# Block loads behind weight loads, a weight sum and a unit's loads in other places, unit 0's bonus work in other levels

## The chip, the core and the metric

The kernel runs on one core of a Trainium2 chip. A core has five engines that work side by side, each through its own instructions in order: TensorE (PE, matrix products into PSUM), VectorE (DVE), ScalarE (ACT), GpSimd (POOL) and SyncE (SP), which here only issues DMAs. Semaphores tie them together. An instruction that waits holds up everything behind it on its engine, and a DMA that waits holds up SP's queue in the same way. The metric is the time of one execution on the device, in microseconds (us), as the median of several runs.

## What is computed

The reference is an RWKV6 attention block followed by a two-layer network with SiLU between the layers, cut here to its core:

```python
for t in range(S):                                   # B, H, S, D = 4, 8, 768, 48
    cur = einsum('bhd,bhe->bhde', u[None] * k[t], v[t])
    y[t] = einsum('bhd,bhde->bhe', r[t], state + cur)
    state = w[t][..., None] * state + einsum('bhd,bhe->bhde', k[t], v[t])
x = y as (3072 tokens, 384)
h = x @ w_in                                         # w_in: 384 x 2048
out = (h * sigmoid(h)) @ w_out                       # w_out: 2048 x 384
```

All data are float32. The recurrence over time is replaced by products inside chunks of 128 tokens, with a state that is carried from chunk to chunk.

## The kernel before

*Units.* The sequence has 6 chunks of 128 tokens, and each is done for two pairs of batches: 12 units, `i` = 0 to 11. The first two (`NTOK = 2`) are special: their inputs come in token by token and are turned on TensorE (`turn_in` L350, then copies L358 to L362), the others come in blocks (`load_blocks`, L106, four DMAs each, twelve calls for a unit) and are turned on VectorE (L338). Two units' inputs fit in `raw`, so the loads for unit `i + 2` go into the room that unit `i` has finished with.

*One unit.* In each of seven levels TensorE makes score products (`scores` or `burst`, L527), VectorE keeps those under a mask (`keep_masked`, L537; for three of them ScalarE copies instead, L556), VectorE multiplies the queries in place (`grow_queries`, L473, or `prepare`, L595), GpSimd the keys (`grow_keys`, L491) and the products of `w` (`product`, L386), and ScalarE moves the odd keys (L461). The queries of a level are overwritten only after the products of that level have read them, and the next level's products need the new ones. The diagonal is a bonus: sums of `r*k*u` (`bonus` L406 to L410, `bonus_sum` L415 and L419) are brought into place (`bonus_spread`: L436 on TensorE in the first two units, in the others by small DMAs into `diag`, L425, ScalarE copies L441 and L443 and a shuffle L444) and written into the scores by VectorE (`bonus_write`, L450, two instructions, `e` = 0 and 1). `reverse_v` reverses `v` of the second batch (L378 on TensorE and a copy L379, later a shuffle L381). Then `y` (L665), `turn_apart` (L628), `dense_x` or `move_x` (L703 with copies L705, or DMAs L715) and `update` (L679) end the unit. In unit 0 the sums of `bonus_spread` lie in `p_w`, a PSUM room that `tail_weight` (L203) uses as well.

*The network.* `up` (L756) makes a piece of the hidden layer from `xt` and `w_in_sb` into `p_h` (two rooms), ScalarE applies SiLU (L762) into `gt`. For the first unit `down` (L775) multiplies with `w_out` as it is. From the second unit on the product is done in seven quarter-size products (`quarter`, L819 and L828), which need sums of `gt` (`sums`, L801) and four sums of quarters of `w_out` (`weight_sums` 0 to 3, L793). `weight_sums(3)` overwrites a quarter of `w_out_sb` that quarter product 5 of unit 1 is the first to need.

*Weights.* Sixteen pieces are loaded (L178) into places that serve several of them, split in two parts on ScalarE (`head_weight` L195 and L197, `tail_weight` L203), joined on VectorE (`join_weight`, L214 and L215) and added on GpSimd (`add_weight`, L227). `join_weight(i)` also issues the load of the piece that takes the place over. Pieces 0 to 5 are loaded at the start, 6 to 11 are issued by the joins of 0 to 5.

*Order.* No scheduler decides: the order on every engine is the order in which the program calls its steps. `do(...)` calls a list of steps. For units 0 and 1 these lists are written by hand (L866 and after); from unit 3 on `mix(i)` returns fourteen groups of steps, and between groups come the steps of the network for the unit before (`ROOM` says how many after each group). `mix` also appends the block loads of unit `i + 2` and the values of unit `i + 1` to the groups from number 3 on, evenly. `beat(n)` issues `n` transposes whose result nobody reads.

Of the kernel before, what the change touches and what calls it, by code (L numbers as in the profile page):

```python
# [38 lines left out]
def kernel(  # L39
# [11 lines left out]
    nc = tc.nc  # L51
# [16 lines left out]
    NTOK = 2  # L68
# [650 lines left out]
    def both(fn, i, *args):  # L719
        return [(fn, i, b, *args) for b in range(NB)]  # L720

    def block_loads(i):
        return [(load_blocks, i, name, g) for name in "wkr" for g in range(4)]

    def mix(i):

        groups = [[*both(turn, i, "w"), (product, i, 0)],
                  [*both(turn, i, "k"), *both(turn, i, "r"), (odd_ones, i)], [(start_levels, i), (prepare_keys, i, 1)],
                  [(prepare, i, 1), *[(product, i, l) for l in range(1, NL)]],
                  [(burst, i, 1), (keep_level, i, 1)], [(keep_level, i, 2), (go_on, i, 2)],  # L730
                  [(prepare, i, 3), (reverse_v, i), (bonus, i, 0)],
                  [(burst, i, 3), (keep_level, i, 3), (bonus_sum, i, 0), (bonus, i, 1), (bonus, i, 2)],
                  [(keep_level, i, 4), (go_on, i, 4)],
                  [(prepare, i, 5), (bonus_sum, i, 1)] + ([(load_rk, i + 1)] if i + 1 < len(units) else []),
                  [(burst, i, 5), (keep_level, i, 5)], [(keep_level, i, 6), (go_on, i, 6), (bonus_spread, i), (bonus_write, i)],
                  both(turn_k, i), [*both(y_state, i), *both(y, i), *both(update, i), (move_x, i)]]

        loads = block_loads(i + NSLOT) if i + NSLOT < len(units) else []
        if i + 1 < len(units):
            loads.insert(len(loads) // 2, (load_values, i + 1))  # L740
        behind = groups[3:]
        for at, group in enumerate(behind):
            group += loads[at * len(loads) // len(behind):(at + 1) * len(loads) // len(behind)]
        return groups
# [89 lines left out]
    def ups(i):  # L834

        steps = [[(up, i, m)] for m in range(FC // 2)]
        for m in range(FH // 2 - 1):

            steps[FH // 2 + 1 + m].append((sums, i, m))
        steps[-1].append((sums, i, FH // 2 - 1))  # L840
        return steps

    def downs(i):
        return [[(quarter, i, x)] for x in range(7)]

    def do(*steps):
        for fn, *args in steps:
            fn(*args)
# [7 lines left out]
    def back(fn, i, *args):  # L856
# [7 lines left out]

    blocks = block_loads(2)
    others = {1: [(clear, 0), (beat, 6)], 2: [(turn, 1, 0, "r"), (head_weight, 0), (beat, 2)],  # L866
              3: [(turn, 1, 1, "r"), (head_weight, 1), (beat, 2)], 4: [(turn, 1, 1, "w"), (reverse_v, 0)],
              5: [(bonus_spread, 0), (bonus_write, 0), (turn, 1, 0, "w")], 6: [*both(turn_in, 1, "k"), *blocks[0:4], (tail_weight, 0)]}
    for l in range(1, NL):
        do((scores, 0, l), *[(grow_keys, 0, l + 1)] * (l + 1 < NL), *others[l])  # L870

    do((bonus, 1, 0), (bonus, 1, 1), (bonus, 1, 2), *both(y, 0), (turn_apart, 0), (join_weight, 0), (add_weight,),
       *blocks[4:8], (product, 1, 0), (tail_weight, 1), (turn, 1, 0, "k"), (join_weight, 1), (dense_x, 0, 0), (turn, 1, 1, "k"),
       (dense_x, 0, 1), (grow_queries, 1, 0), (odd_ones, 1), (tail_weight, 2), *both(turn_k, 0), (head_weight, 2),
       *blocks[8:12], (start_keys, 1, nc.gpsimd, True), (add_weight,), (up, 0, 0), (join_weight, 2),
       (start_keys, 1, nc.gpsimd, False), (add_weight,), (tail_weight, 3), (odd_keys, 1, 1), (head_weight, 3), (grow_keys, 1, 1),
       (scores, 1, 1, (join_weight, 3)), (add_weight,), (up, 0, 1), (tail_weight, 4), (grow_keys, 1, 2), (head_weight, 4),
       (up, 0, 2))


    others = {1: [], 2: [(bonus_sum, 1, 0), (bonus_sum, 1, 1), (load_rk, 2), *both(update, 0)],
              3: [(bonus_spread, 1), (reverse_v, 1), (clear, 1), (load_values, 2)]}

    def piece(i):
# [3 lines left out]
    for m in range(1, 4):  # L888
# [7 lines left out]
    blocks = block_loads(3)  # L896

    others = {0: [(up, 1, 1), (down, 0, 0, 0), *both(turn, 2, "k"), (product, 2, 0), (product, 2, 1)],
              1: [(up, 1, 2), *both(turn, 2, "r"), *[(product, 2, l) for l in range(2, NL)], *blocks[0:3]],
              2: [(down, 0, 0, 1), (odd_ones, 2), (start_keys, 2, nc.gpsimd, True), (grow_queries, 2, 0), *blocks[3:6]],  # L900
              3: [(up, 1, 3), (start_keys, 2, nc.gpsimd, False), (reverse_v, 2), *blocks[6:9]], 4: [(level, 2, 1), (up, 1, 4), *blocks[9:12]],
              5: [(down, 0, 0, 2), (up, 1, 5), (weight_sums, 0)]}
# [5 lines left out]
    blocks = block_loads(4)  # L908
# [10 lines left out]
    for i in range(3, len(units)):  # L919
        steps = downs(i - 2) + ups(i - 1)  # L920
        groups = mix(i)
        if i == NTOK + 1:

            groups[4].append((weight_sums, 3))
        for group, room in zip(groups, ROOM):
            do(*group)
            for step in steps[:room]:
                do(*step)
            steps = steps[room:]
# [32 lines left out]
```

## Time and profile before

| | |
|---|---|
| median of 11 runs | 649.8 us (649.3 to 651.99) |
| profiled execution | 649.36 us, of which the span from the first to the last instruction is 647.6 us |
| instructions | 12887 |
| granted TensorE clock | 1.00 of full speed |
| DMA | 49.21 MB, mean 76 GB/s |

The times in stages, in us (stretch; busy time of TensorE, VectorE, ScalarE, GpSimd):

| stretch | what runs | PE | DVE | ACT | POOL |
|---|---|---|---|---|---|
| 8 to 36 | unit 0 | 26.37 | 22.88 | 21.60 | 23.40 |
| 36 to 127 | units 1 and 2, weights, first of the network | 90.93 | 78.16 | 59.02 | 65.98 |
| 127 to 145 | start of unit 3 | 16.79 | 16.19 | 3.42 | 11.66 |
| 145 to 175 | rest of unit 3 | 29.63 | 16.04 | 7.64 | 9.47 |
| 175 to 647.6 | units 4 to 11 and the end | 469.39 | 294.85 | 107.94 | 166.35 |

A line of the timeline gives start, duration, engine, source line, operation, what is written and read, and in square brackets how long the engine stood idle before and what released it. A line of the waits gives engine, tile and line, the releaser, and the idle time in total, its number and the longest. An engine that is not the last to end may stand idle at no cost. Matmul ends are modelled, so that a matmul group's listed duration reaches a little into the next group.

### The profile page before, as it was taken

What the parts mean: (1) busy time and instruction counts of PE and PEld (TensorE: products, weight loads), DVE (VectorE), ACT (ScalarE), POOL (GpSimd) and SP (SyncE); (2) the same over time, 40 slices, a digit from 0 to 9 for tenths busy, and PEclk for the clock granted to TensorE, in tenths of its full rate; (3) what the DMA queues carried; (4) which work ended last, traced back from release to release, by engine and by line L of the source; (5) the groups of instructions that cost most, each with busy time, mean ns of one, the idle gap of its engine ahead of it and who ended that gap; (6) DMA issues with size and microseconds to landing.
All of it is one profiled execution on the core that took longest, in us unless ns stands there. A gap on an engine that the chain in (4) does not pass through costs nothing.

```text
span 647.6 us, 12887 instructions
## 1 busy us (share of the span) xinstructions
PE 639.4 (99%) x4878; PEld 578.5 (89%) x4878; DVE 433.4 (67%) x737; ACT 203.7 (31%) x408; POOL 282.4 (44%) x356
## 2 busy tenths in 40 slices
PE   8999999999999999999999999999999999999998
PEld 7888876889899899899899899899899989989997
DVE  7879789886487577586586686576576766751031
ACT  6797972212221321330321232231222222131120
POOL 6898388475055154244434426416416505510000
PEclk9999999999999999999999999999999999999999
DMA  9957954444534413514513513523431022000000
GB/s 228 276 94 180 271 126 51 88 78 69 97 53 77 85 36 64 98 30 66 95 29 66 99 26 58 100 33 51 85 62 38 26 50 50 26 3 25 25 0 25
DMA packets 201134, 49.21 MB, mean 76 GB/s; under 512 B 188912, under 2 KB 195952, under 8 KB 201072
## 3 DMA queue, kind: packets, MB, share of 16 engines
q1 hardware_dynamic: 199488, 47.79, 36.2%
q10 hardware_dynamic: 1584, 0.59, 0.4%
q8 instruction: 39, 0.64, 0.4%
q14 instruction: 23, 0.19, 0.1%
HBM read 39.52 MB, written 4.72 MB: 68 GB/s over the span
## 4 chain that ended last, share of the span: by engine, by line
PE 89%; DVE 4%; SPq 2%; POOL 2%; DMA 1%; issue 1%; ACT 1%; POOLq 0%; DVEq 0%; ACTq 0%
PE p_h L756 36%; PE p_o L819 31%; PE p_sc L527 6%; PE p_m L527 3%; PE p_m L775 3%; PE p_m L665 3%; PE p_m L652 3%; PE p_m L639 1%; SPq L106 1%; PE p_sc L679 1%; DMA raw<-in_r_dram 1%; POOL tk L491 1%; DVE score L537 1%; PE p_m L703 0%; DVE tr L473 0%
## 5 line engine op out<-in xcount | busy, mean ns | idle before, releaser
L756 PE MATMUL p_h<-xt,w_in_sb 128*128 128x256 f32 x1152 | 258.5, 382 | 1.1 <-POOL tk L507 0.7
L756 PEld LDWEIGHTS p_h<-xt,w_in_sb 128*128 128x128 f32 x1152 | 215.8, 190 | 33.1 <-POOL tk L507 0.9
L762 ACT ACTIVATE gt<-p_h 128x512 f32<-128x512 f32 x93 | 55.4, 596 | 223.6 <-PE p_h L756 223.5
L491 POOL TENSOR_TENSOR tk<-tk,tw 128x256 f32<-128x256 f32 x144 | 103.1, 739 | 21.3 <-ACT tk L461 15.2
L537 DVE COPY_PREDICATED score<-mask,p_sc 128x512 f32<-128x512 int8 x78 | 64.1, 884 | 60.5 <-PE p_sc L527 60.2
L819 PE MATMUL p_o<-w_out_sb,gt 128*128 128x192 f32 x528 | 90.5, 328 | 0.8 <-DVE w_out_sb L793 0.8
L819 PE MATMUL p_o<-own,temps 128*128 128x192 f32 x528 | 90.3, 328 | 0.4 <-DVE temps L828 0.4
L819 PEld LDWEIGHTS p_o<-w_out_sb,gt 128*128 128x128 f32 x528 | 85.8, 190 | 2.0 <-DVE w_out_sb L793 1.1
L819 PEld LDWEIGHTS p_o<-own,temps 128*128 128x128 f32 x528 | 85.8, 190 | 1.8 <-DVE temps L828 0.7
L684 POOL TENSOR_TENSOR state<-state,tw 128x512 f32<-128x512 f32 x16 | 19.3, 1225 | 119.1 <-PE p_m L652 119.1
L386 POOL TENSOR_TENSOR tw<-tw 128x256 f32<-128x256 f32 (+6 forms) x83 | 38.2, 460 | 56.6 <-DVE tw L338 52.7
L801 DVE TENSOR_TENSOR temps<-gt 128x256 f32<-128x256 f32 x88 | 44.3, 503 | 21.5 <-ACT gt L762 21.5
L461 ACT COPY tk<-tk 128x256 f32<-128x256 f32 x60 | 24.6, 411 | 81.0 <-PE p_sc L527 36.4
L527 PEld LDWEIGHTS p_sc<-tr,tk 48*128 48x128 f32 x640 | 39.2, 186 | 12.1 <-issue 9.1
L473 DVE TENSOR_TENSOR tr<-tr,tw 128x512 f32<-128x512 f32 x53 | 46.0, 869 | 3.3 <-POOL tk L491 1.0
L527 PE MATMUL p_sc<-tr,tk 48*128 48x128 f32 x640 | 47.1, 285 | 0.7 <-POOL tk L491 0.6
L408 POOL TENSOR_TENSOR ruk<-tokens_rk 128x768 f32<-128x768 f32 x10 | 18.6, 1858 | 66.7 <-DVE own_sums L415 66.7
L595 DVE TENSOR_TENSOR tr<-tr,tw 128x512 f32<-128x512 f32 x29 | 39.3, 1354 | 1.3
L537 DVE COPY_PREDICATED score<-mask,p_m 128x512 f32<-128x512 int8 x54 | 35.4, 704 | 0.0
L819 PE MATMUL p_o<-w_out_sb,temps 128*128 128x192 f32 x176 | 30.4, 326 | 0.0
L597 ACT COPY tr<-tr 128x512 f32<-128x512 f32 x29 | 18.4, 634 | 37.3 <-DVE tr L473 36.4
L507 POOL TENSOR_TENSOR tk<-tk,tw 128x128 f32<-128x128 f32 x44 | 29.2, 699 | 1.7 <-ACT tk L497 1.7
(144 smaller groups left out, 734.5 us busy)
## 6 DMA issues: line engine op xcount, KB each, us to landing
w_out_sb<-in_moe_w_in_dram SPq DMA_DIRECT2D x6, 768.0 KB, 6.7
tokens_rk<-in_r_dram SPq DMA_DIRECT2D x20, 192.0 KB, 3.4
tokens_rk<-in_k_dram SPq DMA_DIRECT2D x20, 192.0 KB, 3.9
w_out_sb<-in_moe_w_out_dram SPq DMA_DIRECT2D x4, 768.0 KB, 5.4
own<-in_moe_w_out_dram SPq DMA_DIRECT2D x4, 768.0 KB, 6.8
xt<-yt SPq DMA_DIRECT2D x60, 48.0 KB, 2.0
raw<-in_w_dram SPq DMA_DIRECT2D x80, 32.0 KB, 2.2
raw<-in_k_dram SPq DMA_DIRECT2D x80, 32.0 KB, 2.3
```

The lines of the kernel that those rows point to most:

```text
L386: engine.tensor_tensor(out=up, in0=t[:, :, 0::2], in1=t[:, :, 1::2], op=ALU.mult)
L461: nc.scalar.copy(out=keys(i, X[(l + 1) % 2] * L + c, [4 * c, blocks], [c, 2], [1, c]), in_=keys(i, NP * L + c, [4 * c, blocks], [NP * L + ...
L473: nc.vector.tensor_tensor(out=odd, in0=odd, in1=tw[i][l][:, :, 0::2][:, :, :, None].to_broadcast([128, Q, L >> (l + 1), c]), op=ALU.mult)
L491: nc.gpsimd.tensor_tensor(out=out, in0=have, in1=odd_products(i, l, b, *blocks), op=ALU.mult)
L507: engine.tensor_tensor(out=keys(i, X[1] * L + 3 * b, [4, n], [1, 1]) if own else have, in0=have, in1=odd_products(i, 0, b, [4, n], skip=2 ...
L527: nc.tensor.matmul(bass.AP(tensor=s_p.tensor, offset=s_p.offset, ap=[s_p.ap[0], [apart * L // 2, 2], [1, L // 2]]), lhsT=tk[i][rows, X[l % ...
L537: nc.vector.copy_predicated(out=dst, mask=masks[l][:, :, None].to_broadcast([128, NB, NP, ni, c]), data=sc[e].rearrange("p (b q) (i c) -> ...
L595: nc.vector.tensor_tensor(out=new[:, :, :, 1, :], in0=old[:, :, :, 1, :], in1=tw[i][l][:, :, 0::2][:, :, :, None].to_broadcast([128, Q, L ...
L756: nc.tensor.matmul(p_h[:, a, :], lhsT=w_in_sb[:, c, f * 128:(f + 1) * 128], rhs=xt[i][:, c, :], start=(c == 0), stop=(c == KC - 1))
L762: nc.scalar.activation(out=gt[i, m], in_=p_h, func=AF.Silu)
L801: nc.vector.tensor_tensor(out=out, in0=one, in1=two, op=op)
L819: nc.tensor.matmul(p, lhsT=left(f), rhs=right[:, f, :], start=(f == 0), stop=(f == FH - 1))
```

## The change

Five edits, all of them of places in the order:

1. In unit 0, `bonus_spread(0)` is called in level 3 instead of 5, in the place of a `beat` of two transposes, which goes. The two instructions of `bonus_write(0)` are called one in level 4 and one in level 5, where both were in level 5. `reverse_v(0)` goes from level 4 to level 5, ahead of the second of them.
2. The turns of unit 1: `turn(1, 0, "w")` goes from level 5 to level 6, `turn_in(1, 0, "k")` from level 6 to a place behind `y` of unit 0; the turn-outs of "k" change places, `s` = 1 now comes first.
3. The block loads of unit 2 for "k" and "r" are called later: "k" after the third join of weights, "r" after the piece in the next level. So weight loads 7 to 10 come ahead of them on SP's queue.
4. `mix(3)` puts the loads of unit 5 and the values of unit 4 behind the groups from 10 on, not from 3 on. `mix` of later units stays as it was.
5. `weight_sums(3)` is called second in group 4 of `mix(3)`, between `burst(3, 1)` and `keep_level(3, 1)`, and no longer last.

The number of DMAs and the work of VectorE, ScalarE and GpSimd stay the same. A blank line in `mix` moves the lines from there on by one.

```diff
@@ mix @@
             loads.insert(len(loads) // 2, (load_values, i + 1))
-        behind = groups[3:]
+
+        behind = groups[3 if i > NTOK + 1 else 10:]
         for at, group in enumerate(behind):
@@ unit 0, levels 1 to 6, and unit 1 @@
     others = {1: [(clear, 0), (beat, 6)], 2: [(turn, 1, 0, "r"), (head_weight, 0), (beat, 2)],
-              3: [(turn, 1, 1, "r"), (head_weight, 1), (beat, 2)], 4: [(turn, 1, 1, "w"), (reverse_v, 0)],
-              5: [(bonus_spread, 0), (bonus_write, 0), (turn, 1, 0, "w")], 6: [*both(turn_in, 1, "k"), *blocks[0:4], (tail_weight, 0)]}
+              3: [(turn, 1, 1, "r"), (bonus_spread, 0), (head_weight, 1)], 4: [(turn, 1, 1, "w"), (bonus_write, 0, [0])],
+              5: [(reverse_v, 0), (bonus_write, 0, [1])], 6: [(turn, 1, 0, "w"), (turn_in, 1, 1, "k"), *blocks[0:4], (tail_weight, 0)]}
...
-    do((bonus, 1, 0), (bonus, 1, 1), (bonus, 1, 2), *both(y, 0), (turn_apart, 0), (join_weight, 0), (add_weight,),
-       *blocks[4:8], (product, 1, 0), (tail_weight, 1), (turn, 1, 0, "k"), (join_weight, 1), (dense_x, 0, 0), (turn, 1, 1, "k"),
+    do((bonus, 1, 0), (bonus, 1, 1), (bonus, 1, 2), *both(y, 0), (turn_in, 1, 0, "k"), (turn_apart, 0), (join_weight, 0), (add_weight,),
+       (product, 1, 0), (tail_weight, 1), (turn, 1, 1, "k"), (join_weight, 1), (dense_x, 0, 0), (turn, 1, 0, "k"),
        (dense_x, 0, 1), (grow_queries, 1, 0), (odd_ones, 1), (tail_weight, 2), *both(turn_k, 0), (head_weight, 2),
-       *blocks[8:12], (start_keys, 1, nc.gpsimd, True), (add_weight,), (up, 0, 0), (join_weight, 2),
+       (start_keys, 1, nc.gpsimd, True), (add_weight,), (up, 0, 0), (join_weight, 2), *blocks[4:8],
...
-    others = {1: [], 2: [(bonus_sum, 1, 0), (bonus_sum, 1, 1), (load_rk, 2), *both(update, 0)],
+    others = {1: blocks[8:12], 2: [(bonus_sum, 1, 0), (bonus_sum, 1, 1), (load_rk, 2), *both(update, 0)],
@@ unit 3 @@
-            groups[4].append((weight_sums, 3))
+            groups[4].insert(1, (weight_sums, 3))
```

## The prediction

> **What bounds the kernel now.** I read the page's busy times, then TensorE's waits, then the timelines round each wait that the change touches.
>
> ```profile
> PE 639.4 (99%) x4878; PEld 578.5 (89%) x4878; DVE 433.4 (67%) x737; ACT 203.7 (31%) x408; POOL 282.4 (44%) x356
> ```
>
> TensorE is busy 639.4 of 647.6 us, so 8.2 us of idle time are all that reordering can win, apart from matmuls that are dropped. The waits of TensorE (total us, times, longest) name part of it:
>
> ```profile
> PE p_o L819 <- DVE w_out_sb L793: 0.8, 1, 0.8
> PE p_h L756 <- POOL tk L507: 0.7, 1, 0.7
> ...
> PE p_o L819 <- DVE temps L828: 0.4, 1, 0.4
> PE p_h L756 <- ACT gt L762: 0.4, 1, 0.4
> ```
>
> These four lie at 144.54, 36.05, 136.03 and 173.74 us. From 181 us to the end there are none, so the change is decided before that. The timeline of unit 0 (start us, us, engine):
>
> ```profile
> 20.51 0.44 PE L854 MATMUL p_m<-ident 128*128 128x128 f32 x2
> 20.88 1.16 PE L527 MATMUL p_sc<-tr,tk 48*128 48x128 f32 x16
> ...
> 22.75 1.33 DVE L537 COPY_PREDICATED score<-mask,p_sc 128x512 f32<-128x512 int8 x2
> 23.00 0.91 PE L378 MATMUL p_m<-vq,partial 128*128 128x384 f32 x2
> ...
> 24.93 1.07 PE L436 MATMUL p_w<-own_sums,partial 128*128 128x16 f32 x8
> ...
> 25.13 0.76 DVE L473 TENSOR_TENSOR tr<-tr,tw 128x512 f32<-128x512 f32 x1 [1.04 <-POOL tk L491]
> ...
> 26.43 2.51 DVE L450 COPY_PREDICATED score<-own_mask,p_w 128x1024 f32<-128x1024 int8 x2
> ...
> 26.95 1.16 PE L527 MATMUL p_sc<-tr,tk 48*128 48x128 f32 x16
> ...
> 32.37 2.94 PE L703 MATMUL p_h<-yt,ruk 128*128 128x128 f32 x24
> ...
> 35.35 0.56 DVE L705 COPY xt<-p_h 128x384 f32<-128x384 f32 x1 [0.16 <-PE p_h L703]
> ```
>
> TensorE goes from 20.51 to 35.31 without a gap. Then `up(0, 0)` (L756, 36.05) waits for the copy of `xt`, which ends at 35.91. The wait list names POOL's L507, but that ends at 36.03, after the weight load of this matmul began (36.02), so the copy is the releaser. Unit 3 (same columns):
>
> ```profile
> 138.94 0.36 DVE L828 TENSOR_TENSOR partial<-p_o,partial 128x192 f32<-128x192 f32 x1 [0.83 <-PE p_o L819]
> ...
> 140.04 2.46 DVE L537 COPY_PREDICATED score<-mask,p_sc 128x512 f32<-128x512 int8 x2 [0.74 <-PE p_sc L527]
> ...
> 142.29 2.19 DVE L793 TENSOR_TENSOR w_out_sb<-w_out_sb,own 128x1536 f32<-128x1536 f32 x1
> ...
> 168.68 2.44 SPq L425 DMA_DIRECT2D diag<-own_sums  x4
> 171.12 0.20 ACT L441 COPY both_b<-diag 128x16 f32<-128x16 f32 x1 [3.17 <-DMA diag<-own_sums]
> ```
>
> The last weight sum ends at 144.48, and quarter 5 starts at 144.54. `own_sums` is done at 158.46 (L419), but its DMAs leave SP's queue ten us later, behind block loads; ScalarE stands on them, evicts `gt` late, and TensorE waits at 173.74.
>
> **Unit 0 (levels 3 to 6).** *TensorE.* One `beat` (2 transposes, 20.51 to 20.88) goes: -0.37. In its place comes `bonus_spread`, 0.99 (24.93 to 25.92 before). So scores of level 4 start at 20.51+0.99 = 21.50, 0.62 late. The turn of "w" follows (1.03, as 21.97 to 23.00), then the scores of level 5 at 23.62, and `reverse_v` (0.85) ends at 25.56. *VectorE.* After the scores of level 4 its row L473 comes at 22.14+0.62 = 22.76, and both L537 end at 24.70. Now half a bonus write (2.51/2 = 1.25) stands ahead of the L473 of level 5: it runs 24.65 to 25.90, and L473 ends at 26.66. Before, VectorE idled 1.04 us there. The scores of level 6 need that L473: 26.78, against 26.95. TensorE idles 26.78-25.56 = 1.22, a new gap: the gain of 0.37 and all the shuffling leave only 0.17. ScalarE's four L556 lose the `reverse_v` copy ahead of them and stay hidden. VectorE then ends L537, the other half and the last L537 at about 29.2, before TensorE wants it. 32 transposes of turns (1.73) put `y` at 29.67 (29.84 before). *After `y`.* The third group of 16 transposes of turns, `turn_in(1, 0, "k")`, moves from level 6's cover to behind `y`: 0.86, taken from the 1.73 for 32. So `dense_x` ends at 35.31-0.17+0.86 = 36.00, and `up(0, 0)` starts at 36.74: **+0.69**. The matmuls are the same; the gap is what is added. Bounds: -0.37 if the gap did not form, +1.15 if POOL's L507 is the releaser after all. It waits for ScalarE's copies of the turn of "k" that is now last (done 35.8, L507 then ends at 37.2). I take +0.69, since the start at 36.02 excludes POOL.
>
> **The loads of unit 2.** The same DMAs are issued in another order on SP's queue: weights 6, 7 and 8 together near 39 us, 9 and 10 after the 16 loads of "k" (near 50), 11 after "r" (near 60). Weight 7 left at 49.03 before, and 8 to 11 at 58.76 to 61.4. ScalarE waited 2.17 us for weight 8 at 63.92; that wait goes. TensorE does not stop between 36 and 127 us (90.93 busy of 91), and `y(1)` at 67.56 follows the matmul before it at once, so the gain on the path is 0. What is queued behind: "k" and "r" come about 1 us later by issue, and at worst behind 3 x 768 KB of weights, some 10 us (own<-w_in took 9.8 to land). Their readers, the transposes L338, start at 78.34 and 82.07; "r" was issued by 58.2, so some 14 us are left. Bounds: 0 to -0.45; the latter is the pause in the scores of unit 1 at 45.30 (16 matmuls in 1.63 instead of 1.16), if ScalarE's chain did not move with TensorE. It does move: its copy L705 at 34.01 waits for `dense_x`.
>
> **The last weight sum.** L793 goes ahead of `keep_level(3, 1)`. It can start when L828 ends, 139.30, and takes 2.19: 141.5. Quarter 5 then starts when quarter 4 has ended, 143.70: **-0.84**. Behind it wait the two L537 (2.46): they end at 143.95, not 142.50, and VectorE is 0.53 earlier after that, since 0.74 of its idle time is filled. Their `p_sc` rooms are wanted at 149.1, so 5 us cover it. Bounds: -0.84 to 0 (if the next burst, 149.93, waited instead; its `tr` is ready at 148.4 now, 0.5 earlier then).
>
> **The loads of unit 5.** They go behind group 10 of `mix(3)`. SP's queue is then free at `own_sums`, DMAs land near 162, and the wait of 0.37 at 173.74 goes: **-0.37**. Behind come 16 loads of "w", 16 of "k" and `load_values`: 158.3+2.4+2.7+16x0.49+8x0.49+2.4+8x0.49 = 181.5, where the ten moves of `xt` begin (183.30 before); 16 of "r" end at 197 (194 before). The first reader of this `xt` is at 203.57, of these blocks the transposes near 235. Bounds: -0.37 to 0.
>
> **Sum.** +0.69-0.84-0.37 = -0.52. The profiled execution took 649.36 (span 647.6, 1.76 around it), 0.44 under the median; on the median the forecast is 649.8-0.5 = **649.3 us**.
>
> A rule that speaks against the change: the Trainium skill, "TensorE: Matmul & The Clock Gate", section "HAM oscillation — how this bites in real kernels", says that gaps above about 3.4 us make TensorE slow again, so that taking out filler work is a risk. By this rule a gap of 1.2 us costs nothing, and the sum stays at -0.52; no row here has a gap of that length inside the work.
>
> **Rivals.** *B, faster: the 0.69 is swallowed.* TensorE pauses at 45.30 (0.45) and 136.03 (0.37) for VectorE. If VectorE and ScalarE do not move by 0.69 with TensorE, both pauses shrink: -0.52-0.45-0.37 = -1.34, 648.5 us; if the gap doesn't form either, 647.4. For it: VectorE finishes its bonus writes 0.6 earlier, and weights come earlier. Against: in-order queues tie both engines to `dense_x`. *C, slower: TensorE runs cold after the new gap.* The first 16 transposes took 3.44 us (at 1.36, after 1.36 of idling), the same 16 at 11.08 took 1.97. Each us at the slow rate loses 1-1.97/3.44 = 0.43. From 1.2 us of it on the change loses; two stretches of 3.44 cost 2.9, so 649.8-0.5+2.9 = 652.2; one gives 650.8. For it: a beat is taken out, and no gap of 1.2 us inside the work is shown. Against: after 0.65 of idling at 15.15, the 16 scores took the usual 1.16. *D: the sum doesn't do what it says.* `keep_level(3, 1)` comes 1.45 later, and if that is passed on, the 0.84 comes back at 149.9: 649.8+0.32 = 650.1.
>
> **How the numbers follow.** Forecast 0.49, B 0.25, C 0.15, D 0.11. A change under 0.2% (1.3 us) can't be told from none here. Half of B and its tail, with a part of the forecast's own spread (648.6 to 650.0), lie below 648.5: faster 0.28. Most of C lies above 651.1: slower 0.12. The rest, 0.60, is the same. The range goes from B's end, 647.4, to between C's two prices, 651.2.
>
> **What would show it.** Right: scores of level 4 near 21.5, a TensorE gap near 25.6 to 26.8, L756 near 36.7, no wait of L819 on L793, none on `gt`, and diag's DMAs right behind L419. Wrong: L756 before 36.05, a longer pause at 150, or transposes at 215 ns after 26 us.

## The result and the profile after

| | median (lowest to highest, runs) | profiled execution | span | first scores of level 2 to the end |
|---|---|---|---|---|
| before | 650.26 us (649.18 to 652.92, 50) | 649.36 us | 647.6 us | 631.8 us |
| after | 648.60 us (648.30 to 649.17, 13) | 649.17 us | 647.3 us | 630.7 us |

The ratio of the medians is 0.9972, 95% interval 0.9964 to 0.9981: 1.8 us faster (1.2 to 2.3), where 0.5 was forecast. The 50 runs of before hold the 11 of the first table, so its median is 0.46 higher here than the 649.8 from which the forecast was counted. The two profiled executions differ by only 0.19 us, for two reasons. The profiled execution of before is near the fastest of its runs, and that of after is the slowest of its own. And the scores of level 2 of unit 0, ahead of which no engine's order is changed, start at 16.62 us after and at 15.80 before. These 0.82 us arise in TensorE's first 64 turns, which begin at about the same time but take longer. The first line is of before, the second of after:

```profile
5.16 3.87 PE L350 MATMUL p_m<-ident,raw 128*64 128x128 f32 x64 [0.36 <-DMA raw<-in_k_dram]
...
5.06 4.95 PE L350 MATMUL p_m<-ident,raw 128*64 128x128 f32 x64
```

To compare traces, I count from these scores on: from there to the end it is 631.8 us before and 630.7 after, a gain of 1.1.

The page's first part, of after: busy us, share of the span, instructions.

```profile
PE 639.6 (99%) x4876; PEld 579.4 (90%) x4876; DVE 433.5 (67%) x737; ACT 203.9 (32%) x408; POOL 283.2 (44%) x356
```

The work is the same as before but for the two transposes of the dropped `beat`; otherwise only idle time moved. TensorE's waits of after:

```profile
PE p_sc L527 <- POOL tw L386: 1.0, 1, 1.0
PE p_h L757 <- DVE xt L705: 0.7, 1, 0.7
...
PE p_o L820 <- DVE temps L829: 0.4, 1, 0.4
```

Two lines of before are gone: the wait for the weight sum (0.8) and the wait for `gt` (0.4). One is new, 1.0 at the scores of a level of unit 0. The timeline of unit 0 of after shows where (start us, us, engine; take off 0.82 to lay it beside before):

```profile
21.32 1.06 PE L436 MATMUL p_w<-own_sums,partial 128*128 128x16 f32 x8
...
22.32 1.16 PE L527 MATMUL p_sc<-tr,tk 48*128 48x128 f32 x16
...
25.41 1.28 DVE L450 COPY_PREDICATED score<-own_mask,p_w 128x1024 f32<-128x1024 int8 x1
...
25.52 0.91 PE L378 MATMUL p_m<-vq,partial 128*128 128x384 f32 x2
...
26.59 0.73 DVE L473 TENSOR_TENSOR tr<-tr,tw 128x512 f32<-128x512 f32 x1
...
26.78 1.06 ACT L556 COPY score<-p_h 32x128 f32<-32x128 f32 x4 [1.60 <-DVE score L450]
...
27.47 1.16 PE L527 MATMUL p_sc<-tr,tk 48*128 48x128 f32 x16 [1.03 <-POOL tw L386]
...
28.56 1.97 PE L350 MATMUL p_m<-ident,raw 128*64 128x128 f32 x32
...
36.69 0.56 DVE L705 COPY xt<-p_h 128x384 f32<-128x384 f32 x1 [0.66 <-PE p_h L703]
```

VectorE makes the first bonus write (L450) from 25.41 to 26.69 by the listed durations, and the queries (L473) follow and end at 27.32. The scores of level 6 need these queries: they start at 27.47, after 1.03 of idling. The line names POOL's L386 as releaser, but that group (26.73, 0.65) ends at 27.38, within 0.1 of L473; VectorE's chain is the one that the change made late, and where an experiment below (`c_mend`) makes L473 earlier, the gap shrinks, and POOL's L386 starts only after these scores. The 32 transposes after the gap take 1.97 us, as the same 32 transposes do in before (28.04, 1.97), where no gap stands ahead of them.

`up(0, 0)` (L757 now) starts at 37.39, 20.77 after the scores of level 2; before it was 20.25. Unit 3 of after:

```profile
140.71 1.75 DVE L794 TENSOR_TENSOR w_out_sb<-w_out_sb,own 128x1536 f32<-128x1536 f32 x1
...
142.32 2.87 PE L820 MATMUL p_o<-own,temps 128*128 128x192 f32 x16
142.37 2.45 DVE L537 COPY_PREDICATED score<-mask,p_sc 128x512 f32<-128x512 int8 x2
...
145.02 2.76 PE L820 MATMUL p_o<-w_out_sb,gt 128*128 128x192 f32 x16
...
157.85 1.00 DVE L419 TENSOR_REDUCE own_sums<-ruk 128x8 f32<-128x384 f32 x2
158.41 2.45 SPq L425 DMA_DIRECT2D diag<-own_sums  x4
...
168.23 0.20 ACT L441 COPY both_b<-diag 128x16 f32<-128x16 f32 x1
...
173.59 2.75 PE L757 MATMUL p_h<-xt,w_in_sb 128*128 128x256 f32 x12
```

The weight sum is done at 142.46, 2.6 us before quarter 5 reads its place at 145.02, and no idle time stands in that line. The `diag` DMAs leave the queue from 158.41 on, right behind the instructions that make `own_sums`, and not ten us later; ScalarE's L441 no longer waits for them, and the matmul at 173.59 has no idle time ahead of it.

### The profile page after: what moved, and what is told of

It reads as the page before. It is cut to its first block, busy times and chain, and to the rows that moved or that the text cites. A ratio compares the mean times of both kernels' runs of the same rounds, so it can differ in the third digit from the quotient of the medians.

```text
span 647.3 us, 12884 instructions
## 1 busy us (share of the span) xinstructions
PE 639.6 (99%) x4876; PEld 579.4 (90%) x4876; DVE 433.5 (67%) x737; ACT 203.9 (32%) x408; POOL 283.2 (44%) x356
## 4 chain that ended last, share of the span: by engine, by line
PE 95%; DVE 2%; ACT 1%; POOL 1%; issue 1%; POOLq 0%; DVEq 0%; ACTq 0%
PE p_h L757 38%; PE p_o L820 31%; PE p_sc L527 7%; PE p_m L527 4%; PE p_m L776 3%; PE p_m L665 3%; PE p_m L652 3%; PE p_m L350 1%; PE p_m L639 1%; PE p_sc L679 1%; PE p_m L855 1%; POOL tk L491 1%; PE p_m L703 0%; DVE score L537 0%; PE p_o L527 0%
## 5 line engine op out<-in xcount | busy, mean ns | idle before, releaser
L757 PE MATMUL p_h<-xt,w_in_sb 128*128 128x256 f32 x1152 | 258.4, 382 | 0.7 <-DVE xt L705 0.7
L757 PEld LDWEIGHTS p_h<-xt,w_in_sb 128*128 128x128 f32 x1152 | 215.8, 190 | 32.5 <-POOL tk L507 0.9
L491 POOL TENSOR_TENSOR tk<-tk,tw 128x256 f32<-128x256 f32 x144 | 102.1, 732 | 24.0 <-ACT tk L461 16.6
L386 POOL TENSOR_TENSOR tw<-tw 128x256 f32<-128x256 f32 (+6 forms) x83 | 39.8, 479 | 54.3 <-DVE tw L338 50.4
L473 DVE TENSOR_TENSOR tr<-tr,tw 128x512 f32<-128x512 f32 x53 | 46.3, 873 | 2.9 <-POOL tw L386 1.2
L829 DVE TENSOR_TENSOR partial<-p_o,partial 128x192 f32<-128x192 f32 x33 | 11.6, 353 | 27.6 <-PE p_o L820 27.6
```

What stands on the lines that cost most here:

```text
L386: engine.tensor_tensor(out=up, in0=t[:, :, 0::2], in1=t[:, :, 1::2], op=ALU.mult)
L473: nc.vector.tensor_tensor(out=odd, in0=odd, in1=tw[i][l][:, :, 0::2][:, :, :, None].to_broadcast([128, Q, L >> (l + 1), c]), op=ALU.mult)
L491: nc.gpsimd.tensor_tensor(out=out, in0=have, in1=odd_products(i, l, b, *blocks), op=ALU.mult)
L757: nc.tensor.matmul(p_h[:, a, :], lhsT=w_in_sb[:, c, f * 128:(f + 1) * 128], rhs=xt[i][:, c, :], start=(c == 0), stop=(c == KC - 1))
```

## The experiments

The table has, of each kernel, the median, the ratio to before (on the same chip) with its interval, and three distances of its profiled execution, all from the scores of level 2 of unit 0: to `up(0, 0)`, to quarter product 3 of unit 1's output (behind the pause at 136), and to the end. "Stop" is TensorE's wait for `gt` near 174.

| kernel | median (range, runs) us | ratio [95%] | to `up(0, 0)` | to quarter 3 | to the end | stop |
|---|---|---|---|---|---|---|
| before | | | 20.25 | 120.23 | 631.8 | 0.37 |
| after | 648.60 (648.30–649.17, 13) | 0.9972 [0.9964, 0.9981] | 20.77 | 120.91 | 630.7 | none |
| `s_unit0` | 650.74 (650.03–652.31, 12) | 1.0009 [0.9998, 1.0019] | 20.77 | 120.87 | 633.0 | 0.93 |
| `s_blocks` | 649.74 (648.96–650.60, 12) | 0.9988 [0.9977, 0.9998] | 20.25 | 120.21 | 632.1 | 0.76 |
| `s_late` | 649.74 (648.70–650.62, 12) | 0.9992 [0.9981, 1.0002] | 20.25 | 120.22 | 631.1 | none |
| `s_sum` | 650.54 (648.87–651.88, 12) | 0.9998 [0.9984, 1.0013] | 20.24 | 120.20 | 631.95 | 1.66 |
| `c_34` | 649.00 (648.76–649.87, 11) | 0.9984 [0.9975, 0.9992] | 20.24 | 120.23 | 631.15 | none |
| `c_45` | 648.14 (647.70–648.65, 6) | 0.9969 [0.9957, 0.9980] | 20.25 | 120.22 | 630.0 | none |
| `c_345` | 647.71 (647.43–648.36, 5) | 0.9963 [0.9950, 0.9977] | 20.24 | 120.24 | 630.0 | none |
| `c_mend` | 649.37 (648.95–650.01, 11) | 0.9992 [0.9983, 1.0001] | 21.43 | 121.57 | 631.3 | none |
| `c_all` | 648.71 (648.24–649.17, 6) | 0.9970 [0.9956, 0.9983] | 20.78 | 120.87 | 630.7 | none |
| `u_back` | 648.93 (648.40–649.33, 9) | 0.9966 [0.9953, 0.9979] | 20.86 | 121.01 | 630.9 | none |
| `f_nobeat` | 647.93 (647.27–649.19, 5) | 0.9958 [0.9942, 0.9974] | 19.99 | 120.01 | 629.8 | none |
| `d_dup` | 652.61 (649.43–654.66, 12) | 1.0022 [1.0006, 1.0038] | 20.25 | 125.50 | 635.5 | none |

Rows of one chip: `s_unit0` to `s_sum` (before 650.41 there), `c_34` to `c_mend` (before 650.12), `c_all` to `d_dup` (before 651.10). Medians of different chips are not comparable; their ratios are.

**One part at a time.** `s_unit0` has the edits of unit 0 and of the turns:

```diff
-              3: [(turn, 1, 1, "r"), (head_weight, 1), (beat, 2)], 4: [(turn, 1, 1, "w"), (reverse_v, 0)],
-              5: [(bonus_spread, 0), (bonus_write, 0), (turn, 1, 0, "w")], 6: [*both(turn_in, 1, "k"), *blocks[0:4], (tail_weight, 0)]}
+              3: [(turn, 1, 1, "r"), (bonus_spread, 0), (head_weight, 1)], 4: [(turn, 1, 1, "w"), (bonus_write, 0, [0])],
+              5: [(reverse_v, 0), (bonus_write, 0, [1])], 6: [(turn, 1, 0, "w"), (turn_in, 1, 1, "k"), *blocks[0:4], (tail_weight, 0)]}
...
-    do((bonus, 1, 0), (bonus, 1, 1), (bonus, 1, 2), *both(y, 0), (turn_apart, 0), (join_weight, 0), (add_weight,),
+    do((bonus, 1, 0), (bonus, 1, 1), (bonus, 1, 2), *both(y, 0), (turn_in, 1, 0, "k"), (turn_apart, 0), (join_weight, 0), (add_weight,),
```

and the turns of "k" in exchanged order, as in the change.

> Only the edits of unit 0 and of unit 1's turns are made (bonus_spread, bonus_write, reverse_v, turns). Theory T, the sum of terms: TensorE's new gap ahead of level 6's scores and the 16 transposes behind y cost more than the dropped beat, up(0, 0) comes 0.5 to 0.7 us later counted from the turn of level 3, and the time is 0.5 to 0.7 us over before (ratio about 1.001). Rival V, spread: the kernel before has a wait whose length changes from run to run, and it is not here: runs stay spread over 2 us or more. Rival U: it is the edits of unit 0 that win, the time is at least 0.5 us under before.

`s_blocks` has the loads of unit 2 alone:

```diff
-       *blocks[4:8], (product, 1, 0), (tail_weight, 1), (turn, 1, 0, "k"), (join_weight, 1), (dense_x, 0, 0), (turn, 1, 1, "k"),
+       (product, 1, 0), (tail_weight, 1), (turn, 1, 0, "k"), (join_weight, 1), (dense_x, 0, 0), (turn, 1, 1, "k"),
...
-       *blocks[8:12], (start_keys, 1, nc.gpsimd, True), (add_weight,), (up, 0, 0), (join_weight, 2),
+       (start_keys, 1, nc.gpsimd, True), (add_weight,), (up, 0, 0), (join_weight, 2), *blocks[4:8],
...
-    others = {1: [], 2: [(bonus_sum, 1, 0), (bonus_sum, 1, 1), (load_rk, 2), *both(update, 0)],
+    others = {1: blocks[8:12], 2: [(bonus_sum, 1, 0), (bonus_sum, 1, 1), (load_rk, 2), *both(update, 0)],
```

> Only the block loads of unit 2 are moved behind the weight loads. Theory T: 0 within 0.2 us, since TensorE does not stop between 36 and 127 us; ScalarE's wait of 2.17 us for weight 8 near 64 us is gone. Rival V: this part takes away a wait that varies from run to run (weights that land late), so its runs lie within 1 us of each other and their median is 0.5 to 1 us under before, although the profiled executions show no difference.

`s_late` has the loads of unit 5 alone:

```diff
-        behind = groups[3:]
+        behind = groups[3 if i > NTOK + 1 else 10:]
```

> Only the loads of unit 5 are moved behind group 10 of mix(3). Theory T: TensorE's stop before up(2, 7) near 174 us is gone, worth 0.6 us by the comparison of the two traces (0.37 by the row of matmuls, 0.61 by the row of weight loads). Rival V: that stop varies from run to run with the pace of SP's queue, so this part wins 1 us or more and the spread of its runs is under 1 us.

`s_sum` has the weight sum alone:

```diff
-            groups[4].append((weight_sums, 3))
+            groups[4].insert(1, (weight_sums, 3))
```

> Only the last weight sum is called ahead of keep_level(3, 1). Theory T: -1.07 us by the comparison of the two traces (0.84 by the row of matmuls, 1.13 by the row of weight loads); spread as before. Rival D of the prediction: 0, the wait comes back at the next burst near 150 us. Rival V: no part in the spread, runs still over 2 us apart.

Measured: the part of unit 0 costs 0.52 at `up(0, 0)` and 0.64 at quarter 3, where the whole change costs 0.52 and 0.68, so this part alone makes that loss. The other three leave both distances as they were, within 0.03. The loads of unit 5 alone remove the stop and gain 0.7 to the end, and 0.5 by the ratio, where the interval (−0.1 to 1.2) includes 0. The loads of unit 2 alone bring 0.8 us (0.1 to 1.5) by the ratio, though nothing in the profiled execution, which is 0.3 longer to the end (its stop is 0.76 and not 0.37). The surprise is the weight sum: alone it brings nothing, neither by the ratio nor to the end (631.95). Its timeline in unit 3 tells why:

```profile
139.13 1.75 DVE L793 TENSOR_TENSOR w_out_sb<-w_out_sb,own 128x1536 f32<-128x1536 f32 x1
...
156.27 1.00 DVE L419 TENSOR_REDUCE own_sums<-ruk 128x8 f32<-128x384 f32 x2
...
168.77 2.44 SPq L425 DMA_DIRECT2D diag<-own_sums  x4
...
171.22 0.20 ACT L441 COPY both_b<-diag 128x16 f32<-128x16 f32 x1 [4.45 <-DMA diag<-own_sums]
...
173.84 2.42 PE L756 MATMUL p_h<-xt,w_in_sb 128*128 128x256 f32 x10 [1.66 <-ACT gt L762]
```

`own_sums` is done about 1.2 us earlier than before (157.27 by this line against 158.46), yet the `diag` DMAs leave the queue at 168.77, where they left at 168.68 before: the queue is held by the block loads, which don't care how early TensorE is. So TensorE arrives earlier at the same wait, and its stop grows from 0.37 to 1.66. All that the sum gains is lost 30 us later.

The stop also differs between kernels that have before's order throughout unit 3: 0.37 in before, 0.93 in `s_unit0`, 0.76 in `s_blocks`. Counted from quarter 3, the `diag` DMAs leave 32.65, 33.20 and 33.02 us later in these three (168.68 less 136.03, 170.00 less 136.80, 169.93 less 136.91), and the stop follows. In `s_sum` it is 32.82, which lies among them: the queue took no notice of the sum.

**Parts together.** `c_34`, `c_45` and `c_345` put the diffs above together by their numbers (3 the loads of unit 2, 4 the loads of unit 5, 5 the weight sum).

> Both edits of loads (unit 2's block loads behind weights; unit 5's loads late in mix(3)), nothing else. Theory S (two waits for DMAs whose length changes from run to run, one at up(2, 7) near 174 us, one at y(1) near 67 us when weight 8 lands late): the two parts add up or more, about -1.1 us against before, and the runs lie within 1 us. Rival R (the spread comes from the input loads of the first 12 us alone): spread of 2 us or more stays, -0.6 us.

> Unit 5's loads late and the weight sum early, without the block loads and without unit 0. Theory S: the stop before up(2, 7) cannot swallow the weight sum's gain any more, so the profiled execution, counted from the scores of level 2 of unit 0, ends 1.7 us earlier than before's (1.07+0.64); the median is 1.5 to 2 us under before, with spread left from weight 8. If the sum's gain was nothing by itself, 0.6 us.

> The change without its unit 0 part. Theory S: 0.5 to 0.6 us faster than the whole change, so 2.2 to 2.4 us under before (ratio 0.9965), runs within 1 us. Rival U (unit 0's edits also bring something that the first 36 us don't show): no faster than the whole change, ratio 0.997 or above.

The two edits of loads together (`c_34`) gain 1.0 by the ratio, near what they gain alone (0.8 and 0.5). With the queue freed, the sum counts: `c_345` is 1.3 us under `c_34` in the median on the same chip (649.00 to 647.71), and 1.15 to the end in the trace. `c_45` gains 2.0 us by its ratio, where its two parts alone gain 0.5 and 0.1: the loads of unit 5 are worth little for themselves, but they let the other through. The loads of unit 2 on top (`c_45` to `c_345`) make no difference to the end in the trace (630.0 both) and 0.43 in the median, where the intervals overlap. `c_345` is the change without its part of unit 0, and its median is the lowest on its chip, 2.4 us under before by the ratio (1.5 to 3.2).

**Mending unit 0.** `c_mend` keeps the whole change but makes the first bonus write only behind the queries of level 5, so that L473 is not late, and puts `turn_in(1, 0, "k")` back ahead of `y`:

```diff
-              3: [(turn, 1, 1, "r"), (bonus_spread, 0), (head_weight, 1)], 4: [(turn, 1, 1, "w"), (bonus_write, 0, [0])],
-              5: [(reverse_v, 0), (bonus_write, 0, [1])], 6: [(turn, 1, 0, "w"), (turn_in, 1, 1, "k"), *blocks[0:4], (tail_weight, 0)]}
+              3: [(turn, 1, 1, "r"), (bonus_spread, 0), (head_weight, 1)], 4: [(turn, 1, 1, "w")],
+              5: [(reverse_v, 0), (bonus_write, 0, [1])], 6: [(turn, 1, 0, "w"), (turn_in, 1, 1, "k"), (turn_in, 1, 0, "k"), *blocks[0:4], (tail_weight, 0)]}
...
-        do((scores, 0, l), *[(grow_keys, 0, l + 1)] * (l + 1 < NL), *others[l])
+        do((scores, 0, l, *[(bonus_write, 0, [0])] * (l == 5)), *[(grow_keys, 0, l + 1)] * (l + 1 < NL), *others[l])
...
-    do((bonus, 1, 0), (bonus, 1, 1), (bonus, 1, 2), *both(y, 0), (turn_in, 1, 0, "k"), (turn_apart, 0), (join_weight, 0), (add_weight,),
+    do((bonus, 1, 0), (bonus, 1, 1), (bonus, 1, 2), *both(y, 0), (turn_apart, 0), (join_weight, 0), (add_weight,),
```

> The whole change with unit 0 mended: the first half of the bonus write is called behind grow_queries of level 5 and not ahead of it, and turn_in(1, 0, k) goes back ahead of y. The gap theory: TensorE's gap of 1.03 us ahead of the scores of level 6 is gone or under 0.2, y waits for VectorE instead by 1 us at most, up(0, 0) comes 20.0 us after the scores of level 2 (20.25 before, 20.77 with the change): 0.7 us faster than the change, 2.4 us under before. If VectorE's queue is the bound at y: no faster than c_345.

It got worse: 21.43 to `up(0, 0)`. The gap ahead of level 6 shrinks to 0.46, but others open. The timeline of `c_mend`:

```profile
25.82 1.30 DVE L450 COPY_PREDICATED score<-own_mask,p_w 128x1024 f32<-128x1024 int8 x1
...
26.05 1.16 PE L527 MATMUL p_sc<-tr,tk 48*128 48x128 f32 x16 [0.46 <-DVE tr L473]
...
27.21 1.06 ACT L556 COPY score<-p_h 32x128 f32<-32x128 f32 x4 [2.87 <-PE p_sc L527]
...
28.29 0.48 ACT L379 COPY vq<-p_m 128x384 f32<-128x384 f32 x1
...
28.82 1.09 PE L350 MATMUL p_m<-ident,raw 128*64 128x128 f32 x16 [0.59 <-ACT vq L379]
...
30.12 1.09 PE L350 MATMUL p_m<-ident,raw 128*64 128x128 f32 x16 [0.20 <-ACT tw L362]
```

ScalarE's four copies L556 write into the same half of `score` as L450, so they come behind it: they start at 27.21, when L450 has ended (27.12), after 2.87 of idling. (The line names the scores of level 6 as releaser, but these copies read `p_h`, which the scores of level 5 had filled earlier.) Behind them in ScalarE's queue is the copy L379 that frees the room of `reverse_v` in `p_m`, and the transposes that want a room there wait for it, 0.59. In the change itself L556 waits 1.60 for L450 in the same way. So the new place of `bonus_write` ties three engines together, and delaying it only moves the wait.

**The turn behind `y`, and the beat.** `c_all` is the whole change once more. `u_back` is the whole change with only the turn put back ahead of `y` (above, `turn_in(1, 0, "k")` in level 6 and not behind `y`). `f_nobeat` is `c_345` without the two transposes of level 3:

```diff
-              3: [(turn, 1, 1, "r"), (head_weight, 1), (beat, 2)], 4: [(turn, 1, 1, "w"), (reverse_v, 0)],
+              3: [(turn, 1, 1, "r"), (head_weight, 1)], 4: [(turn, 1, 1, "w"), (reverse_v, 0)],
```

> The whole change again, on the chip of this call, as the measure for the next two. Theory S: 1.4 to 1.9 us under before, runs within 1.1 us.

> The whole change, but turn_in(1, 0, k) called ahead of y again, behind the other turns of level 6. If the gap ahead of level 6's scores is the cost in unit 0: the same matmuls follow the gap in another order, and the time is that of the whole change within 0.2 us. If the move of these 16 transposes behind y is the cost (0.86 by the row of 32 transposes): 0.6 to 0.9 us faster than the whole change.

> The change without its unit 0 part, and without the beat of two transposes in level 3. TensorE goes without a gap from there to dense_x, so up(0, 0) comes 19.9 us after the scores of level 2 (20.25 before) and the time is 0.3 to 0.4 us under c_345, 2.6 us under before (ratio 0.996). If VectorE's last L537 of unit 0 holds y: 0 to 0.1. If the beat keeps TensorE's rate up: transposes and scores after it take longer than 1.16 us for 16 and the time is above c_345's.

`u_back` has the same gap of 1.03 ahead of level 6 and comes to `up(0, 0)` at 20.86, no earlier than the change (20.78 in `c_all`). So moving the 16 transposes only shifts work that has to be done anyway. The gap, which is there with and without that move, is what costs. `f_nobeat` comes there at 19.99, 0.25 earlier than `c_345`, and is 0.2 shorter to the end: the beat can be had without the rest. By its ratio it is not told apart from `c_345` (0.9958 and 0.9963). Both are ahead of the change (0.9972 and 0.9970) too, `c_345` by 0.7 and `f_nobeat` by 0.9 us to the end in the traces; the intervals of the ratios overlap.

**What a late weight costs.** The loads of unit 2 gain in the median and not in the profile. `d_dup` is `c_45` with four DMAs doubled ahead of weight 8, so that it comes surely late:

```diff
-       *blocks[8:12], (start_keys, 1, nc.gpsimd, True), (add_weight,), (up, 0, 0), (join_weight, 2),
+       *blocks[8:12], blocks[11], (start_keys, 1, nc.gpsimd, True), (add_weight,), (up, 0, 0), (join_weight, 2),
```

> As c_45 (no block loads moved, no unit 0), with the last four block loads of unit 2 issued twice, so that weights 8 to 11 leave SP's queue some 2.5 to 4 us later. Theory S (y(1) near 67 us stands right behind ScalarE's wait for weight 8): TensorE stops ahead of y(1) for about that delay less 0.1, and the time rises by 2 to 4 us over c_45. Rival: the weights have cover, ScalarE's wait for weight 8 grows but TensorE does not stop, and the time is c_45's within 0.3 us; then the block loads' part in the spread is not a late weight.

Its timeline:

```profile
68.59 0.88 ACT L195 ACTIVATE temps<-w_out_sb 128x768 bf16<-128x768 bf16 x1 [6.14 <-DMA w_out_sb<-in_moe_w_out_dram]
...
71.64 0.74 ACT L556 COPY score<-p_sc 64x256 f32<-64x256 f32 x2
...
72.05 1.98 PE L665 MATMUL p_m<-score,vt 128*64 128x128 f32 x16 [3.73 <-ACT score L556]
73.81 1.68 PE L665 MATMUL p_m<-score,vq 128*64 128x128 f32 x16
```

and the same place in before:

```profile
63.92 0.92 ACT L195 ACTIVATE temps<-w_out_sb 128x768 bf16<-128x768 bf16 x1 [2.17 <-DMA w_out_sb<-in_moe_w_out_dram]
...
67.04 0.75 ACT L556 COPY score<-p_sc 64x256 f32<-64x256 f32 x2
...
67.56 1.09 PE L665 MATMUL p_m<-score,vt 128*64 128x128 f32 x16
```

`y(1)` does hang on weight 8: L195 waits for its DMA, the copies L556 stand behind it on ScalarE, and `y(1)` needs the first of them. In `d_dup` TensorE stops 3.73 us for it, and the kernel is 5.5 us over `c_45` to the end in the trace (635.5 and 630.0) and some 3.5 by the two ratios (1.0022 and 0.9969). Ten of its twelve runs took 651.85 us or more, with a granted clock of 0.995 to 0.997 over the span; the other two took 649.43 and 649.69, at 0.999 and 1.000. So this long stop seems to be absent from some executions of one kernel. Of the 22 runs of before on that chip one has such a clock, the longest (653.48 at 0.997). In before that first copy ends near 67.42 (67.04 and half of 0.75), 0.14 ahead of `y(1)`. Counted from the scores of level 2, L195 got weight 8 at 48.12, 47.86, 48.01 and 48.08 in the profiled executions of before, `s_late`, `s_sum` and `c_45`, none of which stopped: in these four it moves by only 0.26 us, and the first copy ends 0.14 to 0.41 ahead of `y(1)`. An execution in which it lands 0.2 us later than in before would stop. In `s_unit0`, whose loads are in before's order too, there is no wait for weight 8 at all:

```profile
62.43 0.92 ACT L195 ACTIVATE temps<-w_out_sb 128x768 bf16<-128x768 bf16 x1
...
65.65 0.76 ACT L556 COPY score<-p_sc 64x256 f32<-64x256 f32 x2
...
68.34 1.09 PE L665 MATMUL p_m<-score,vt 128*64 128x128 f32 x16
```

That is 46.50 after the scores of level 2, and the first copy ends 2.3 ahead. So with the same order of loads weight 8 came at least 1.3 us earlier there than in any of the other four; how late it can come, no trace but that of `d_dup` shows. With the loads moved, L556 starts at 64.97 in `c_345` and `y(1)` at 67.66: the first copy ends 2.3 us ahead. So edit 3 takes away a wait that can be there in some executions only. That this happens in enough runs of before to make the 0.4 (`c_45` to `c_345`) to 0.8 us (`s_blocks`) by which edit 3 lowers the median is an inference: no profiled execution of before's order of loads was caught in it.

The spread of the runs fits, in the main. The kernels with edits 3 and 4 both (`c_34`, `c_345`, `c_all`, `u_back`, `c_mend`, after) have from 0.9 to 1.1 us between the lowest and the highest run. `s_blocks`, `s_late`, `s_unit0` and `s_sum` have 1.6, 1.9, 2.3 and 3.0, and before from 2.1 to 4.9 in its four sets of runs. Against it speak `c_45` (0.95 in 6 runs), which lacks edit 3, and `f_nobeat` (1.9 in 5 runs), which has both. The numbers of runs differ too, 5 to 13 against 22 to 50 of before, and more runs reach further out, so this comparison supports the inference only weakly.

## Why the prediction was right, and where it was not

The time, 648.60, lies in the range, and the signs that it named came true; the gain is 1.3 us more than forecast. By its own steps:

- **Unit 0, +0.69.** Right in mechanism and nearly in size: scores of level 4 at 21.50 (22.32 less 0.82 is 21.50), L473 late behind the bonus write, a new gap of 1.03 (1.22 foretold), `up(0, 0)` 0.52 later (0.69), 0.64 to 0.68 later by quarter 3, since the pause in unit 1's scores then costs a further 0.14 (from their start to the next group 1.70 after, 46.63 to 48.33, and 1.56 before, 45.30 to 46.86). Three details were wrong. The dropped `beat` was put at 0.37; `f_nobeat` shows 0.25 for it. The four L556 do not "stay hidden": they wait 1.60 for L450, which costs nothing in the change and did in `c_mend`. And the 16 transposes behind `y` are not the cause of anything (`u_back`).
- **The last weight sum, −0.84.** Mis-sized: from the start of quarter 4 to the burst behind quarter 6 TensorE took 9.11 us before (140.83 to 149.94) and takes 8.00 after (142.32 to 150.32), so 1.11 came free; to the end it is 1.15 (`c_34` to `c_345`). The 0.84 was the idle time in the matmul row; the row of the weight loads of the same instruction says 1.1, and that is near what came free. The step was also costed with 2.19 for L794, which took 1.75 in its new place. The view of before's weight loads has the two idle times:

```profile
PEld p_o L819 <- DVE w_out_sb L793: 1.1, 1, 1.1
...
PEld p_h L756 <- ACT gt L762: 0.6, 1, 0.6
```

- **The loads of unit 5, −0.37.** The same: 0.6 in the weight loads' row, 0.7 to the end in `s_late`, where 0.37 was taken from the matmul row; and in two more executions with before's order in unit 3 the stop was 0.76 and 0.93. The moves of `xt` begin at 184.42 and not at 181.5, which no wait shows: from 181 us to the end TensorE has none after either. The DMAs follow L419 and the wait on `gt` is gone, as foretold. But the step was costed as if it stood alone. What the forecast did not say is that it is the condition of the step before it: without it, the sum's gain goes into the stop at 174 (`s_sum`), whose DMAs leave at a time that TensorE does not set.
- **The loads of unit 2, 0.** Right for the profiled executions, where `c_45` and `c_345` need the same 630.0, and wrong for the medians by about half a us (0.8 alone, with an interval of 0.1 to 1.5, and 0.4 on top of the others). The sentence that `y(1)` follows the matmul before it at once was true, but the cover was 0.14 us, on a DMA whose landing, counted from the scores of level 2, differed by more than 1.6 between five executions with this order of loads. The times of the loads behind were mis-sized, at no cost in this trace: "k" and "r" were to come about 1 us later by issue, but the last "r" was issued by 66.4, not 58.2, still 17 us ahead of its reader L338 at 83.55.
- **On the median.** Here is the step that failed: the sum of one execution, with short waits for DMAs, was set on the median of the runs. By the traces the parts give +0.7 −1.1 −0.7 = −1.1, which is the 631.8 to 630.7 measured. By medians they give +0.6 (the ratio of after, 0.9972, against that of `c_345`, 0.9963), −1.3 (`c_34` to `c_345`), −0.5 (`s_late`) and −0.4 to −0.8 (the loads of unit 2): −1.6 to −2.0, against −1.8 measured, each term uncertain by some 0.6. So of the 1.3 that were missed, 0.6 lie in terms read too small. The rest, some 0.7, no trace shows. Waits that are longer in the median than in the profiled execution of before would give it: that one had the shortest stop at 174 of three (0.37) and no stop at weight 8. But by medians the loads of unit 5 alone gain 0.5, no more than by the trace. So it stays open what makes the rest.

The rivals: B (a gain of 1.3) has nearly the time but not the reason, since the pause at 136 stayed at 0.4 and the one in unit 1's scores grew by 0.14, the 0.69 was not swallowed, and the gain came from larger sums. C is false: after the gap of 1.03 the 32 transposes took 1.97 us, and the granted clock from 25 to 30 us was 1.00. D is false at its place, 149.9, where there is no wait; but its kind is real, as a gain that comes back in a later wait, 25 us further on and only where edit 4 is left out.

## What to carry to other kernels

Where several waits stand in a row on the path, a wait that ends at a time which a DMA queue sets can swallow what is gained ahead of it, as the stop at 174 did in `s_sum`, so free that queue first or cost the two edits together. Read the size of a TensorE stop in the row of the weight loads as well as in that of the matmuls: here 1.1 and 0.6 were nearer to what came free than 0.8 and 0.4. It is no rule: at the new gap of unit 0 the row of the weight loads says 1.62, while from L378 (25.52) to the scores (27.47) it is 1.95 us, against 0.84 before (23.00 to 23.84), so the gap took 1.11, near the 1.03 of the matmuls. Only the distance between two fixed groups of matmuls in both traces says it surely. And look at how much time lies between a DMA's reader and the path, not only at whether it waits in the one profile: a cover of 0.14 us beside a landing time that moves by more can be a cost in some of the runs, which the median holds and one profile does not show.

## What was not expected of the hardware

In `d_dup` the stop of 3.73 us was followed by slow matmuls: 16 of L665 took 1.98 and the next 16 took 1.68 us, against 1.09 and 1.04 in the same place of before. In stretches of the span of `d_dup` (busy time of TensorE, its instructions, the granted clock, the DMA share, GB/s):

```profile
60.00:65.00 5.00, 5.00 (x40) 1.00 0.38 60
...
71.00:76.00 5.00, 3.95 (x48) 0.66 1.17 262
76.00:80.00 4.00, 4.00 (x61) 1.00 0.76 130
```

The clock is 0.66 from 71 to 76 us and full again after. So a stop of this length costs more than itself: 1.5 us more for these 32. Gaps of 1.03 (after) and 1.66 us (`s_sum`) were not followed by it. The Trainium skill, "TensorE: Matmul & The Clock Gate", section "HAM oscillation — how this bites in real kernels", names gaps above about 3.4 us as those that slow TensorE; all three gaps agree with it.

The start of the work moved between executions of kernels that are the same up to there: the scores of level 2 of unit 0 began between 15.75 and 16.70 us. TensorE's first 64 turns go with it: they took 3.86 us in `s_sum` (scores at 15.75), 4.33 in `c_all` (16.27) and 5.03 in `s_blocks` (16.70), though they began at 5.08, 5.02 and 5.10. Why their rate differs was not tried. And the weight sum, one VectorE instruction, took 1.75 us in its new place (after, `s_sum`) and 2.16 and 2.19 in its old one (`s_late`, before). GpSimd's instructions beside it move the other way: six L386 took 3.92 us beside the new place in after and 2.36 in before, four L491 beside the old place 4.01 in before and 2.61 in after. Which of the two engines holds up the other, and why, was not tried.
